# Attention feeding a two-layer network on one core: the value products in 64x64 quarters, in two parts around the next scores

## The chip, the cores and the metric

The kernel runs on one core of a Trainium2 chip. The metric is the device time of one execution in microseconds (us), the median of a few runs; lower is better. The engines are named as in the profile: PE (matrix products; PEld is its weight load), DVE (elementwise and reductions), ACT (activations and copies), POOL (elementwise, selections) and SP (it issues the transfers).

## The reference

Batch 8, 8 heads, sequence 576, head width 64. Each query sees the 128 keys up to and including its own, with a distance bias per head; the result is the input of a network with 512 inputs, 2048 hidden units and 512 outputs.

```python
scores = scale * np.matmul(q, k.transpose(0, 1, 3, 2))
bias = slopes[:, None, None] * (-np.abs(rel).astype(np.float32))[None, :, :]
mask = (rel >= 0) & (rel < window)                    # window = 128
scores = np.where(mask, scores + bias[None], -1000000000.0)
attn = softmax(scores)                                # max, exp, sum, divide
attn_out = np.matmul(attn, v)
x = attn_out.transpose(0, 2, 1, 3).reshape(B * S, H * D)
out = (np.maximum(x @ w_in, 0.0) ** 2) @ w_out
```

## The kernel before, in words

The 4608 tokens are cut into nine chunks of 512, the heads into four pairs. A *couple* q is one chunk and one head pair (q = 4 x chunk + pair, 36 couples); it holds two *segments* of 256 queries, and a segment two groups i of 128 queries for each of the two heads j. A 64-query block sees three 64-key blocks: two of them always in view in whole or in part (the *base*, 128 columns) and one more that shares the place of the block it replaces (the *extra*, 64 columns). The softmax works on a folded 128x128 square per group: `base` copies the base scores from PSUM with ACT, `fold` merges the extra scores under a mask with DVE, then come the row maxima (`top`, DVE), the exponentials (ACT), the sums, and the normalization (`norm`, POOL). `squares` transposes the result on DVE in 32x32 blocks, sends it through DRAM (`way`) and reads it back, and two selections on POOL split it into `own` (keys of the group's own 128-key block) and `prev` (keys of the block before). In `own`, a key only meets queries that stand at or behind it, in `prev` only queries that stand before it in the next block, so one 64x64 quarter of each 128x128 square is all zeros.

The value products (`mix_squares`, L338) multiply those squares with the values: weights of 128 keys x 64 head columns, 128 query columns at a time, two squares added up per group, and the two heads j side by side in the two column halves of the array. `scores` (L392) multiplies 64-row by 64-column pieces of queries and keys, all four quarters of the array in use. The bulk of the work is the network in split precision: `gemm1` (L194) is 12 products of 128x128 weights with 512 columns per hidden block f and chunk, `gemm2` (L223) another 12. ACT takes the Relu from `gemm1`'s bank g, and later steps square and split it.

PSUM has eight banks: two for `sc` (the scores of a couple, S), one for `at` (the value result X), one for `g1` (gemm1's g, and the base scores G of a couple's second segment), four for the accumulators of `gemm2`. Every pool but the last holds one buffer.

The first 150 us or so are ordered by a planner (`start`, with its table of costs and due times); it does the first chunks' attention and the network's chunk 0, and is not touched by the change. From then on PE's order is the written one of the main loop, and the other engines' order comes from a scheduler with priorities. Every eighth half step of the loop holds a *visit*, right behind a `gemm1`: the value products of the old couple q-1 (`back`: `values`, then the copy `high` on ACT and the remainder `low` on DVE, which make that couple's part of the network's input xu), then the scores of the new couple q (`front`), then `gemm2` goes on. Couples 8 to 35 have their value products in such visits: 28 visits, 27 of which also hold the scores of a new couple. In `scores` both heads of the second segment write the one bank G; a POOL no-op (the *turn*) stands between the heads, since the two row halves of the array must not write one bank at a time. A couple whose queries stand at the start of a sequence of 576 has fewer key blocks (`late`); this holds for one or two 64-query blocks of each chunk.

## Time and profile before

| what | value |
|---|---|
| time, median of 3 runs | 956.27 us (956.26 to 956.36) |
| span of the profiled execution, first to last instruction | 954.1 us |
| PE busy | 945.6 us (99%) |
| PEld / DVE / ACT / POOL busy | 795.7 / 499.0 / 417.5 / 215.3 us |
| granted TensorE clock | 1.000 |
| value products, L338 | 1024 records, 63.0 us |
| scores, L392, of the tiles s, g and at | 1648 records |

The profiled execution has no timer of its own beside its span; the timed runs are 2.1 us longer than the span, which is what lies ahead of the first instruction and behind the last. One matrix product of full fp32 stands as two records. A record's duration contains the way through the array, so records overlap; what a piece costs is read from the distance between starts.

### The profile page before, as it was taken

The page shows a single profiled execution, that of the slowest core. Times are in us where ns is not written, and L with a number is a line of the kernel's source. Part 1 is how long each engine was busy: PE and PEld are TensorE (multiplying, and loading weights), DVE is VectorE, ACT ScalarE, POOL GpSimd, SP SyncE. Part 2 cuts the span into 40 slices and gives each one's busy share as a digit, 9 for nine tenths or more (in the row PEclk, how much of TensorE's full clock was granted, in tenths as well). Part 3 has the DMA queues.
Part 4 walks back from the last instruction along what each step waited for, and adds up shares of the span by engine and source line. Part 5 has one row for each costly group of instructions (what it writes and reads, how often), then busy time and mean ns, then how long its engine had stood idle before and what let it go on. Part 6 is the DMA issues. An engine that isn't in the chain of part 4 may idle for free.

```text
span 954.1 us, 17229 instructions
## 1 busy us (share of the span) xinstructions
PE 945.6 (99%) x6388; PEld 795.7 (83%) x6392; DVE 499.0 (52%) x1334; ACT 417.5 (44%) x1107; POOL 215.3 (23%) x254
## 2 busy tenths in 40 slices
PE   9899999999999999999999999999999999999998
PEld 5688888888888888888888888888888888888886
DVE  6998864455545455444544454455555444433222
ACT  7898743333444444434433343344344343332222
POOL 4123331222222222222222222221212222220000
PEclk9999999999999999999999999999999999999999
DMA  9974423322433333222433232333422231111001
GB/s 348 404 274 153 146 68 119 83 66 66 124 85 83 84 88 107 73 77 73 128 83 83 74 110 72 83 83 92 119 71 72 72 96 45 45 45 45 1 1 44
DMA packets 72883, 95.10 MB, mean 100 GB/s; under 512 B 8032, under 2 KB 41952, under 8 KB 72800
## 3 DMA queue, kind: packets, MB, share of 16 engines
q1 hardware_dynamic: 72368, 93.36, 32.9%
q8 instruction: 50, 0.82, 0.4%
q10 hardware_dynamic: 432, 0.66, 0.2%
q14 instruction: 33, 0.27, 0.1%
HBM read 67.76 MB, written 26.21 MB: 98 GB/s over the span
## 4 chain that ended last, share of the span: by engine, by line
PE 95%; DMA 4%; ACT 0%; issue 0%; DVE 0%; SPq 0%; DVEq 0%
PE acc L223 42%; PE g L194 42%; PE at L338 6%; PE s L392 2%; PE g L392 2%; DMA raw<-in_dram 2%; DMA wide<-in_dram 1%; DMA qk<-in_dram 1%; PE at L392 0%; ACT raw L165 0%; ACT t L426 0%; PE acc L291 0%; ACT t L419 0%; ACT o L229 0%; DVE xu L304 0%
## 5 line engine op out<-in xcount | busy, mean ns | idle before, releaser
L194 PE MATMUL g<-xu,w 128*128 128x512 f32 x1728 | 423.2, 394 | 0.8 <-issue 0.8
L194 PEld LDWEIGHTS g<-xu,w 128*128 128x128 f32 x1728 | 344.1, 209 | 56.2 <-issue 1.7
L223 PE MATMUL acc<-hh,w 128*128 128x512 f32 x1152 | 385.9, 396 | 0.0
L223 PEld LDWEIGHTS acc<-hh,w 128*128 128x128 f32 x1152 | 223.9, 194 | 44.6 <-issue 2.4
L207 DVE TENSOR_TENSOR r<-r 128x512 f32<-128x512 f32 x129 | 104.4, 810 | 245.4 <-ACT r L204 244.2
L204 ACT ACTIVATE r<-g 128x512 f32<-128x512 f32 x144 | 85.9, 597 | 325.8 <-PE g L194 322.7
L223 PE MATMUL acc<-hl,w 128*128 128x512 f32 x576 | 226.6, 393 | 0.0
L326 POOL TENSOR_SCALAR_AFFINE_SELECT pp<-pp 128x512 f32<-128x512 f32 x128 | 107.1, 841 | 210.6 <-DMA pp<-way 171.6
L213 DVE TENSOR_TENSOR hl<-r,hh 128x512 fp32r<-128x512 f32 x144 | 109.4, 760 | 68.3 <-ACT hh L211 67.6
L262 POOL TENSOR_TENSOR t<-t,nm 128x512 f32<-128x512 f32 x64 | 82.8, 1294 | 263.5 <-DVE nm L259 155.9
L223 PEld LDWEIGHTS acc<-hl,w 128*128 128x128 f32 x576 | 112.0, 194 | 19.8
L251 ACT ACTIVATE t<-t,nm 128x128 f32<-128x128 f32 x256 | 100.0, 393 | 56.7 <-DVE nm L244 56.6
L211 ACT CAST hh<-r 128x512 fp32r<-128x512 f32 x144 | 89.0, 618 | 76.1 <-DVE r L207 74.5
L438 DVE COPY_PREDICATED t<-cst,s 64x256 f32<-64x256 int32 x100 | 44.5, 445 | 40.8 <-ACT t L426 22.4
L313 DVE STREAM_TRANSPOSE pp<-t 128x512 f32<-128x512 f32 x64 | 45.2, 707 | 38.7 <-POOL t L262 38.5
L338 PEld LDWEIGHTS at<-pp,v 128*64 128x64 f32 x1024 | 55.2, 137 | 11.2 <-issue 10.8
L338 PE MATMUL at<-pp,v 128*64 128x128 f32 x1024 | 63.0, 276 | 0.0
L244 DVE CUSTOM_DVE_ANT_0 t<-t,cst 128x128 f32<-128x128 f32 x256 | 59.0, 293 | 1.0
L251 ACT ACTIVATION_READ_ACCUMULATOR t<-t,nm 128x1 f32 x256 | 48.2, 188 | 0.0
L392 PE MATMUL s<-qk 64*64 64x64 f32 (+2 forms) x1168 | 46.3, 251 | 0.8 <-ACT raw L165 0.8
L392 PEld LDWEIGHTS s<-qk 64*64 64x64 f32 x1168 | 41.9, 133 | 1.0 <-ACT raw L165 1.0
L428 POOL MEMSET t<- 64x128 f32 (+1 forms) x44 | 9.9, 227 | 137.5 <-PE g L392 128.5
(63 smaller groups left out, 472.2 us busy)
## 6 DMA issues: line engine op xcount, KB each, us to landing
raw<-in_dram SPq DMA_DIRECT2D x32, 512.0 KB, 8.7
way<-pp SPq DMA_DIRECT2D x256, 64.0 KB, 1.8
pp<-way SPq DMA_DIRECT2D x64, 256.0 KB, 2.8
qk<-in_dram SPq DMA_DIRECT2D x32, 320.0 KB, 3.5
v<-in_dram SPq DMA_DIRECT2D x32, 320.0 KB, 2.9
qk<-in_dram SPq DMA_DIRECT2D x38, 256.0 KB, 4.1
out_dram<-o SPq DMA_DIRECT2D x35, 256.0 KB, 4.3
v<-in_dram SPq DMA_DIRECT2D x3, 256.0 KB, 4.9
```

What stands on the lines that cost most here:

```text
L194: nc.tensor.matmul(g, w, xs[cc][:, part], start=i == 0, stop=i == 11)
L204: self.relu = nc.scalar.activation(r, g, AF.Relu)
L207: nc.vector.tensor_tensor(r, r, r, op=ALU.mult)
L211: nc.scalar.copy(hh, r)
L213: nc.vector.tensor_tensor(hl, r, hh.bitcast(F32), op=ALU.subtract)
L223: nc.tensor.matmul(self.acc[m], w, h, start=(f == 0 and i == 0), stop=(f == NF - 1 and i == 2))
L244: self.nc.vector.tensor_tensor_reduce(self.t[:, m], self.t[:, m], self.K.nrel(2 * self.p + m // 2), -0.125, BIG, ALU.add, ALU.min, self.nm ...
L251: return self.nc.scalar.activation(self.t[:, m], self.t[:, m], AF.Exp, bias=nm[:, m : m + 1], scale=-1.0, accum_out=nm[:, 4 + m : 5 + m],)
L262: self.nc.gpsimd.tensor_tensor(self.t, self.t, self.nm[:, 8:12].unsqueeze(2).to_broadcast([128, 4, 128]), op=ALU.mult)
L326: nc.gpsimd.affine_select(to, self.own, pattern=[[-32 * sign, 4], [0, 4], [-sign, 32]], compare_op=op, fill=0.0, base=0, channel_multiplie ...
L338: self.nc.tensor.matmul(self.X[r, o : o + 128].rearrange("p (a c) -> p a c", a=4), v[:, 2 * sg + k, r], src[:, :, 2 * j + i], start=sg == ...
L392: mm = nc.tensor.matmul(to, qk[r, q0 : q0 + 64], qk[r, k0 : k0 + 64 * n], start=True, stop=True, skip_group_check=True,)
```

## The change

The visit is written anew as one function, `visit`, for couples 8 to 35.

- The value products go in quarters: 64 keys x 64 head columns as weights, and 64 or 128 query columns. `own` and `prev` are cut by the key half r; for r = 0, `prev` is used for the first 64 queries only and `own` for all 128, for r = 1 `prev` for all and `own` for the last 64. The other quarters, which are zero, are left out. A couple has 32 products for 16 before, with 3072 columns in sum for 2048 before.
- The two row halves of the array write different banks: in the first part, segment 0 takes key half 0 into bank 0 of S, segment 1 key half 1 into bank 1; in the second part the halves change over and add to what stands there. The result X is now columns 0 to 255 of both banks of S.
- The new couple's scores stand between the two parts. Its extra scores go to columns 256 to 511 of S, its base scores, of both segments, to a new two-bank tile `big`. Head j writes bank j. All extras come first, then all bases. The turn (a POOL no-op) now waits for the last extra, and the second part waits for the turn.
- `gemm1` uses the second bank of `big` in place of `g1`; the pools `at` and `g1` are closed when the planner's part is over.
- The copy and the remainder that make xu (`out`) are recorded behind the new couple's base copies and folds, ahead of its maxima; `base` of the first segment now reads `big` and no longer S.

```diff
@@ Kern
+        self.later = ExitStack()
+        pp = lambda name: self.later.enter_context(tc.tile_pool(name=name, bufs=1, space=PSUM))
+        self.at, self.g1 = pp("at"), pp("g1")
+    def join(self, ctx):
+        self.later.close()
+        self.big = ctx.enter_context(self.tc.tile_pool(name="big", bufs=1, space=PSUM))
@@ gemm1
-        g = self.g1.tile([128, 512], F32, name="g")
+        g = self.big.tile([128, 2, 512], F32, name="g")[:, 1] if self.big else self.g1.tile([128, 512], F32, name="g")
@@ Segment
+    def quarters(self, S, r):
+        K, sg = self.K, self.sg
+        v, rows = K.v[self.c, self.p], slice(64 * r, 64 * r + 64)
+        for i in range(2):
+            parts = ((self.prev, 2 * sg + i, 0, 2 + 2 * r), (self.own, 2 * sg + i + 1, 2 * r, 4))
+            for src, k, a, e in parts if r == 0 else parts[::-1]:
+                for j in range(2):
+                    cols = slice(64 * j, 64 * j + 64)
+                    to = S[cols, sg, 128 * i + 32 * a : 128 * i + 32 * e].rearrange("p (a c) -> p a c", c=32)
+                    yield to, v[rows, k, cols], src[rows, a:e, 2 * j + i]
@@ Couple
+    def quarters(self):
...
+                for part, s, i in ((part, s, i) for part in (extra, base) for s in range(2) for i in range(2)):
...
+        for _, j, h, extra, to, q, k, n in sorted(todo, key=lambda y: y[:3]):
+            r = slice(64 * j, 64 * j + 64)
+            yield extra, to, qk[r, q : q + 64], qk[r, k : k + n]
@@ Couple.front
-        self.scores(self.K.g1, "g")
...
-        self.both[0].soft()
@@ Couple
-    def back(self):
-        self.values()
-        self.high()
-        self.low()
+    def out(self, S):
...
+        self.X = S[:, :, 0:256]
...
+def visit(K, old, new):
+    nc, mm = K.nc, K.nc.tensor.matmul
+    S = K.sc.tile([128, 2, 512], F32, name="s")
+    def phase(rows, first):
+        made = []
+        for n, pair in enumerate(zip(*(G.quarters(S, r) for G, r in zip(old.both, rows)))):
+            for to, w, x in pair:
+                made.append(mm(to, w, x, start=first and n < 2, stop=not first, skip_group_check=True))
+        return made
+    last = phase((0, 1), True)[-1]
+    if new:
+        new.S, new.B = S, K.big.tile([128, 2, 512], F32, name="g")
+        for extra, to, w, x in new.quarters():
+            made = mm(to, w, x, start=not extra, stop=True, skip_group_check=True)
+            last = made if extra else last
+    turn = nc.gpsimd.nop()
+    K.tc.add_manual_dep(turn.ins, last.ins.name, SYNC, reason="halves of the keys change banks")
+    for made in phase((1, 0), False)[:2]:
+        K.tc.add_manual_dep(made.ins, turn.ins.name, SYNC, reason="halves of the keys change banks")
+    if new:
+        new.front()
+    old.out(S)
+    if new:
+        new.both[0].soft()
@@ main loop
+        K.join(ctx)
...
-                        if q - 1 in pairs:
-                            pairs.pop(q - 1).back()
...
-                            C.front()
-                            C.turn(0)
...
+                        if q - 1 in pairs:
+                            visit(K, pairs.pop(q - 1), late)
+                        if late:
+                            late.turn(0)
```

How the change moves instructions on PE, in the first visit of the loop: a row is one product or a run of like ones, with the output tile, the inputs, the columns and the count; xu and w are the operands of `gemm1`, pp holds the squares, v the values, qk the queries and keys. Before (the middle of the scores is left out):

```order
L194 MATMUL g<-xu,w_379 128x512 x12
L338 MATMUL at<-pp,v 64x128 x16
L392 MATMUL g<-qk 64x128 x2
L392 MATMUL s<-qk 64x192
L392 MATMUL s<-qk 64x128
L392 MATMUL g<-qk 64x128 x2
...
L392 MATMUL g<-qk 64x128
L392 MATMUL s<-qk 64x64
L223 MATMUL acc<-hh,w_282 128x512
```

And with the change:

```order
L200 MATMUL g<-xu,w_379 128x512 x12
L539 MATMUL s<-pp,v 64x64 x4
L539 MATMUL s<-pp,v 64x128 x4
L539 MATMUL s<-pp,v 64x64 x4
L539 MATMUL s<-pp,v 64x128 x4
L546 MATMUL s<-qk 64x64 x13
L546 MATMUL g<-qk 64x128
L546 MATMUL s<-qk 64x64
L546 MATMUL g<-qk 64x128 x13
L539 MATMUL s<-pp,v 64x64 x4
...
L539 MATMUL s<-pp,v 64x128 x4
L229 MATMUL acc<-hh,w_282 128x512
```

The 16 value products of 128 rows became two groups of 16 quarters, and the scores, which alternated between g and s, now write s first and g behind it.

On ACT, in a visit near the middle of the run (t holds the folded squares, r and hh belong to the network, g and s are the PSUM tiles). Before:

```order
L204 ACTIVATE r_4204<-g_4191 128x512 [waits DVE_49,PE_49]
L211 CAST hh_4205<-r_4204 128x512 [waits DVE_49]
L477 CAST xu_4228<-at_4211 128x512 [waits PE_49]
L426 COPY t_4265<-g_4237 64x2x128 [waits PE_49,Pool_49]
L426 COPY t_4265<-g_4237 128x2x128
L419 COPY t_4263<-s_4236 128x512 [waits DVE_49,PE_49,Pool_49]
L251 ACTIVATE t_4263,nm_4264<-t_4263,nm_4264 128x128 [waits DVE_49,Activation_49]
```

And with the change:

```order
L210 ACTIVATE r_4393<-g_4380 128x512 [waits DVE_49,PE_49]
L217 CAST hh_4394<-r_4393 128x512 [waits DVE_49]
L468 COPY t_4470<-g_4422 64x2x128 [waits PE_49,Pool_49]
L468 COPY t_4470<-g_4422 128x2x128
L461 COPY t_4468<-g_4422 128x512 [waits Pool_49]
L527 CAST xu_4481<-s_4405 128x512 [waits DVE_49,PE_49]
L257 ACTIVATE t_4468,nm_4469<-t_4468,nm_4469 128x128 [waits DVE_49,Activation_49]
```

The copy that makes xu moved from ahead of the base copies to behind them, and waits for DVE's folds; the base copy of the first segment lost its wait for DVE.

On DVE, the same visit with the change, from the last maximum of the first segment on (nm holds maxima and sums):

```order
L250 ISA t_4468,nm_4469<-t_4468,cst_93 128x128
L250 ISA nm_4469 128x1
L528 TENSOR_TENSOR xu_4481<-s_4405,xu_4481 128x512 [waits Activation_49]
L264 TENSOR_SCALAR nm_4469<-nm_4469 128x4 [waits Activation_49]
L265 RECIPROCAL nm_4469<-nm_4469 128x4 [waits DVE_49]
L319 STREAM_TRANSPOSE pp_4495<-t_4468 128x4x4x32 [waits DMAHW2_49,DMAHW3_49,DMAHW1_49,DMAHW7_49,DMAHW0_49,Pool_49]
L213 TENSOR_TENSOR r_4530<-r_4530 128x512 [waits Activation_49]
```

Before, the remainder that makes xu (L480) stood ahead of the folds and the maxima, directly behind the network's own remainder (L213); now it stands behind all eight maxima.

More of the change, by code (lines that the diff above doesn't have):

```diff
@@ L407, in bases @@
     def bases(self, s):
+        parts = lambda x: x.rearrange("p j (i c) -> p j i c", i=2)
+        if self.B is not None:
+            return parts(self.B[:, :, 256 * s : 256 * s + 256]), parts(self.S[:, :, 256 + 128 * s : 384 + 128 * s])
         if s == 0:
@@ L411, in bases @@
             return x[..., 0:128], x[..., 128:192]
-        parts = lambda x: x.rearrange("p j (i c) -> p j i c", i=2)
         return parts(self.G.rearrange("p (j c) -> p j c", j=2)), parts(self.S[:, :, 384:512])
+    def quarters(self):
+        B, S = self.B, self.S
+        todo = []
+        for h in range(2):
+            base, extra = (h, h + 1), (2 - 2 * h,)
+            for j in range(2):
+                at = 0
+                for part, s, i in ((part, s, i) for part in (extra, base) for s in range(2) for i in range(2)):
+                    blocks = [x for x in part if x >= self.both[s].late.get(2 * i + h, 0)]
+                    if not blocks:
+                        continue
+                    n, a = len(blocks), 64 * (blocks[0] - part[0])
+                    if part is extra:
+                        to = S[64 * h : 64 * h + 64, j, 256 + 128 * s + 64 * i : 320 + 128 * s + 64 * i]
+                    else:
+                        to = B[64 * h : 64 * h + 64, j, 256 * s + 128 * i + a : 256 * s + 128 * i + a + 64 * n]
+                    u = 4 * s + 2 * i + h
+                    todo.append((at, j, h, part is extra, to, 64 * u + 640 * s, 256 + 64 * (u + blocks[0]), 64 * n))
+                    at += 64 * n
+        qk = self.K.qk[self.both[0].c, self.both[0].p]
+        for _, j, h, extra, to, q, k, n in sorted(todo, key=lambda y: y[:3]):
+            r = slice(64 * j, 64 * j + 64)
+            yield extra, to, qk[r, q : q + 64], qk[r, k : k + n]
     def base(self, s):
@@ L742, in tile_attn_moe @@
                         if q < 4 * NCH:
[L743 to L746 removed]
+                            late = pairs[q] = Couple(K, q)
+                        if q - 1 in pairs:
+                            visit(K, pairs.pop(q - 1), late)
+                        if late:
+                            late.turn(0)
                 if t % 2 == 0 and n < NF * NCH:
```

11 lines of the change are left out of this document (7 added, 4 removed).

## The prediction

> **What bounds the kernel now.** I read the page first: the share of each engine, the granted clock and the chain of waits.
>
> ```profile
> PE 945.6 (99%) x6388; PEld 795.7 (83%) x6392; DVE 499.0 (52%) x1334; ACT 417.5 (44%) x1107; POOL 215.3 (23%) x254
> PEclk9999999999999999999999999999999999999999
> PE acc L223 42%; PE g L194 42%; PE at L338 6%; PE s L392 2%; PE g L392 2%; DMA raw<-in_dram 2%; DMA wide<-in_dram 1%; DMA qk<-in_dram 1%; PE at L392 0%; ACT raw L165 0%; ACT t L426 0%; PE acc L291 0%; ACT t L419 0%; ACT o L229 0%; DVE xu L304 0%
> ```
>
> PE works without a gap at the full clock, and nearly the whole chain is PE. So the time of the main loop is the sum of PE's own steps: what makes a visit shorter makes the kernel shorter, as long as no new wait comes up on PE. Next I read PE's groups with shapes kept apart, for the tiles in question, and the timeline of PE around one visit.
>
> ```profile
> L338 PE MATMUL at<-pp,v 128*64 128x128 f32 x1024 | 63.0, 276 | 0.0
> L392 PE MATMUL s<-qk 64*64 64x64 f32 x704 | 37.3, 218 | 0.0
> ```
>
> ```profile
> 309.09 2.92 PE L194 MATMUL g<-xu,w 128*128 128x512 f32 x12
> 311.94 1.97 PE L338 MATMUL at<-pp,v 128*64 128x128 f32 x32
> 313.83 0.33 PE L392 MATMUL g<-qk 64*64 64x64 f32 x2
> ...
> 315.21 0.51 PE L223 MATMUL acc<-hh,w 128*128 128x512 f32 x1
> 315.55 0.40 PE L223 MATMUL acc<-hl,w 128*128 128x512 f32 x1
> ```
>
> Neither group waited for anything (0.0). The 32 records of the values take 1.89 us (311.94 to 313.83), the scores 1.38 (to 315.21). A record's 276 or 218 ns holds its way through the array and is no cost; the distance of starts is. Windows cut from the first record of a piece to the first of the next give the values once and the scores once for each of chunks 2 to 8 (there are 3 visits of chunk 2 and 4 of each other; one stands for its chunk).
>
> ```profile
> 157.84:159.73 1.89, 1.89 (x33) 1.72 (x32) 0.69 (x1) 1.03 (x2) 0.00 (x0) 1.00 0.00 0
> 159.73:161.21 1.48, 1.48 (x55) 1.32 (x53) 1.26 (x2) 0.71 (x2) 0.30 (x1) 1.00 0.31 40
> 236.95:238.33 1.38, 1.38 (x55) 1.29 (x53) 1.13 (x2) 0.71 (x2) 0.40 (x2) 1.00 0.23 30
> 339.46:340.92 1.46, 1.46 (x51) 1.31 (x49) 1.21 (x2) 0.70 (x2) 0.30 (x1) 1.00 0.26 46
> 442.15:443.52 1.37, 1.37 (x54) 1.30 (x52) 1.12 (x2) 0.71 (x2) 0.40 (x2) 1.00 0.27 57
> 544.63:546.09 1.46, 1.46 (x51) 1.30 (x49) 1.21 (x2) 0.70 (x2) 0.30 (x1) 1.00 0.27 35
> 647.33:648.80 1.47, 1.47 (x54) 1.39 (x53) 1.23 (x2) 0.70 (x2) 0.20 (x1) 1.00 0.32 56
> 750.29:751.79 1.50, 1.50 (x59) 1.42 (x57) 1.26 (x2) 0.70 (x2) 0.20 (x1) 1.00 0.37 59
> ```
>
> **What a quarter costs.** The scores already run in 64x64 quarters, so their steps price the new value products. PE's timeline in a visit of chunk 8, where g and s take turns in all four quarters:
>
> ```profile
> 750.29 0.33 PE L392 MATMUL g<-qk 64*64 64x128 f32 x2
> ...
> 750.45 0.28 PE L392 MATMUL g<-qk 64*64 64x128 f32 x2
> ...
> 750.66 0.28 PE L392 MATMUL g<-qk 64*64 64x128 f32 x2
> ...
> 751.32 0.23 PE L392 MATMUL s<-qk 64*64 64x64 f32 x2
> ...
> 751.37 0.29 PE L392 MATMUL s<-qk 64*64 64x64 f32 x4
> ...
> 751.49 0.29 PE L392 MATMUL s<-qk 64*64 64x64 f32 x3
> ```
>
> From 750.45 to 750.66 lie two steps of four records of 128 columns: 0.105 us a step. For the values, 16 steps of two records in 1.89 us, less 0.05 for a longer first step (750.29 to 750.45 is 0.16) and 0.10 for the end, give 0.109; I take 0.109. From 751.32 to 751.49 two quarters start six records of 64 columns, three steps: 0.057; I take 0.058. So a step takes as long as its columns, for two tiles of 128x64 and for four of 64x64 alike. Bounds for the 64 columns: 0.055 (half of 128) and 0.109 (no cheaper than 128); the row is at the lower one.
>
> The formula has a check. In the scores each quarter of the array has a stream of its own; the longest decides. A full stream is 768 columns in records of two per product: 4 extras, 2 x 4 x 0.058 = 0.46, and 4 bases, 2 x 4 x 0.109 = 0.87, in sum 1.34. With 0.05 for the first step and 0.11 for the end that is 1.50: chunk 8 has 1.50, chunk 7 1.47. With 704 columns it is 1.22 + 0.16 = 1.38: chunks 3 and 5 have 1.38 and 1.37, but chunks 2, 4 and 6 have 1.48, 1.46, 1.46. I put their 0.08 to 0.10 to the turn between the heads in bank G (an estimate by difference).
>
> **The change part by part.**
>
> *Values.* One part has 16 quarters in four streams: per stream four records of 64 columns and four of 128, 4 x 0.058 + 4 x 0.109 = 0.67. Two parts: 1.34. Before it was 1.89 with its own start and end. The start and end now come once per visit, 0.16, since parts and scores share one shape; the jump from `gemm1` to a visit stays as it is.
>
> *Scores.* All are now split into 64 and 128 columns and no bank is shared, so only the longest stream counts: 1.34 (chunks 7, 8), 1.23 (3, 5: a base of 64 columns for 128), 1.22 (2, 4, 6: an extra is missing).
>
> *Sum per visit*, before less after: chunk 2: 1.89 + 1.48 - (0.16 + 1.34 + 1.22) = 0.65; chunk 3: 3.27 - 2.73 = 0.54; 4: 3.35 - 2.72 = 0.63; 5: 3.26 - 2.73 = 0.53; 6: 0.63; 7: 3.36 - 2.84 = 0.52; 8: 3.39 - 2.84 = 0.55. Over the visits: 3 x 0.65 + 4 x (0.54 + 0.63 + 0.53 + 0.63 + 0.52 + 0.55) = 15.6 us. The last visit has no scores, so its turn lies open between the parts. The turn as it is today, in a visit of chunk 4 (the last record of head 0 in bank G, then the first of head 1):
>
> ```profile
> 337.56 1.97 PE L338 MATMUL at<-pp,v 128*64 128x128 f32 x32
> ...
> 339.85 0.27 PE L392 MATMUL g<-qk 64*64 64x128 f32 x1
> ...
> 340.34 0.32 PE L392 MATMUL g<-qk 64*64 64x128 f32 x1
> ```
>
> 0.49 us from start to start, so 0.4 of wait: 0.05 + 1.34 + 0.4 + 0.11 = 1.90, nothing won there.
>
> *What hides the new waits.* All times from a visit's start, for the first visit of chunk 3 (it starts at 235.06, 1.89 ahead of the window of its scores), where the most hangs on them. ACT, DVE and PE before:
>
> ```profile
> 235.16 0.60 ACT L204 ACTIVATE r<-g 128x512 f32<-128x512 f32 x1 [3.11 <-PE g L194]
> ...
> 238.45 1.03 ACT L426 COPY t<-g 64x128 f32<-64x128 f32 x3 [0.79 <-PE g L392]
> 240.52 0.92 ACT L426 COPY t<-s 128x256 f32<-128x256 f32 x3 [1.04 <-DVE t L438]
> ```
>
> ```profile
> 237.89 0.69 DVE L480 TENSOR_TENSOR xu<-at,xu 128x512 fp32r<-128x512 f32 x1
> 239.51 0.90 DVE L438 COPY_PREDICATED t<-cst,s 64x256 f32<-64x256 int32 x2 [0.92 <-ACT t L426]
> 241.47 0.45 DVE L438 COPY_PREDICATED t<-cst,s 64x256 f32<-64x256 int32 x1 [1.06 <-ACT t L426]
> ...
> 242.47 0.29 DVE L244 CUSTOM_DVE_ANT_0 t<-t,cst 128x128 f32<-128x128 f32 x1
> 242.69 0.08 DVE L244 DVE_READ_ACCUMULATOR2_ANT nm<- 128x1 f32 x1
> ```
>
> ```profile
> 241.24 2.95 PE L194 MATMUL g<-xu,w 128*128 128x512 f32 x12
> ```
>
> (1) The base products write the tile that `gemm1`'s result just left, so they wait for its Relu, which ends at 0.70. Before, the values (1.89) covered that; now the first part (0.72) and three rounds of extras (6 x 0.058) do, to 1.07. Cover left: 0.37; without it the Relu's delay would stand on PE in each visit, with the second part and `gemm2` queued behind. (2) The turn: the last extra starts at about 1.13, plus 0.49 is 1.62; the bases run to 1.95. (3) The next `gemm1` needs the tile back, so both base copies must be done: scores end at 1.95, copies start 0.23 later as now (238.45 against 238.22), 1.03 + 0.92 make 4.1, and the next `gemm1` starts at 6.18 - 0.54 = 5.64. The first segment's copy no longer waits for the fold (1.04 in the row). (4) xu: folds end at 4.17 + 1.00 = 5.17 (241.47 to 242.47), the copy of 0.59 at 5.8, the eight maxima (0.22 each, 242.47 to 242.69) at 6.9, the remainder (0.69) at 7.6. Only in the first visit of a chunk does the next `gemm1` use this xu, its remainder in the eleventh product: 5.64 + 10 x 0.23 (2.95 less the last record's 0.39, over 11 steps) = 7.95. Cover 0.35. (5) The squares of the old couple must be ready at the start of a visit:
>
> ```profile
> 332.02 3.84 POOL L326 TENSOR_SCALAR_AFFINE_SELECT pp<-pp 128x512 f32<-128x512 f32 x4 [5.39 <-DMA pp<-way]
> ```
>
> They end at 335.86, 1.7 ahead of the visit at 337.56. The loop gets some 0.6 shorter per visit, but the chain behind the scores starts 1.3 earlier too, so nothing is late. SP and POOL issue the same work; the loads wait for the end of the visit's PE work and are for a couple two visits on.
>
> So the sum is 15.6 us: the span of 954.1 goes to 938.5. The median of the runs is 2.1 above the span, which the change leaves alone: **940.7 us**.
>
> **The rivals.**
>
> *A wait eats part of it.* Covers (1) and (4) are 0.35 us, and I have drawn them from starts and ends without the handover from engine to engine. If a wait of 0.2 to 0.4 shows in each visit, 27 x 0.3 = 8 us come back: 949. If it shows only at the six chunk starts, 6 x 0.4 = 2.4: 943. For it: two of the covers are thin. Against: they are there. Chance 0.16, most of it small.
>
> *PE's issue becomes the bound.* A visit now issues some 120 products with as many weight loads in 2.7 us, 22 ns a pair; before it was 84 in 3.3, 39 ns. What the trace shows is one burst behind a long wait in the planner's part:
>
> ```profile
> L392 PEld LDWEIGHTS s<-qk x36: 129/133/135, 41.6 to 42.7; 64*64 64x64 f32 x36
> L392 PE MATMUL s<-qk x36: 214/218/344, 41.6 to 42.8; 64*64 64x64 f32 x24, 64*64 64x128 f32 x8, 64*64 64x192 f32 x4
> L392 PE MATMUL at<-qk x12: 267/269/320, 41.7 to 42.8; 64*64 64x128 f32 x12
> ```
>
> 48 pairs in 1.2 us are 25 ns a pair, and that burst may have been bound by its columns. At 25 ns a visit would take 3.0: 27 x 0.3 = 8 us come back, 949. Chance 0.05. The Trainium skill ("TensorE: Matmul & The Clock Gate", section "Wait — 56ns, not 53.3ns?") says that with hardware decoding off the sequencer spends about 62 ns on each matrix product, which would be the bound for small ones. By that rule a visit of 120 products would take an estimated 7.4 us and the kernel would be slower by more than 100; the burst above does not agree with it, so the rule gets no chance of its own.
>
> *Slower: the quarters of the values don't run four at a time.* Unlike the scores, they add to a bank, and two quarters read different 32-column runs of the same rows. If only two of four ran together, a part would take 1.34 and a visit 0.75 longer than before (1.34 lost, 0.59 won): 27 x 0.75 + 1.3 for the last visit = 22 us, 978. It decides from the point where a part takes over 0.96. For it: no row shows an adding quarter. Against: the values before add as well, read the same runs, and keep 0.109. Chance 0.05.
>
> *The change doesn't do what it says*, with the turn or a bank wait holding up each part so that the gain is just used up: 0.6 of new waits per visit, 956. It would take a wait of more than both thin covers together. Chance 0.04.
>
> **How the numbers follow.** The forecast has 0.70, the rivals 0.16, 0.05, 0.05, 0.04. A measurement of this kernel can tell 0.2%, 1.9 us, from no change. Faster: 0.70 + 0.16 + 0.05 = 0.91; the same 0.03; slower 0.06. The range: the lower end is the sum with steps of 0.105 and 0.055, which takes another 0.12 a visit (parts 1.28 for 1.34, scores 0.06 less), 27 x 0.12 = 3.2 us: 937.5. The upper end takes in the waits that eat a part, to 949, with a little less than the full 8 us: 948.0.
>
> **What would show it.** Right: the values' two parts take 0.67 to 0.72 us each, the scores between them 1.2 to 1.35, a visit with scores 2.7 to 2.85, the gap from `gemm1` to the visit and the steps of `gemm1` and `gemm2` are unchanged, and no idle time on PE has ACT, DVE or POOL behind it. Wrong: a first base record that starts later than 1.1 into the visit (Relu), a step in the eleventh product of the first `gemm1` of a chunk (xu), a gap ahead of the second part (turn), or steps of 64 columns over 0.06 (issue, or quarters that take turns). The forecast falls if two adding quarters in one column half can't run together.

## The result, and the profile after

| | before | with the change |
|---|---|---|
| time, median of 4 runs | 956.26 us (956.00 to 956.36) | 941.21 us (940.99 to 941.43) |
| ratio, 95% interval | | 0.984 (0.983 to 0.986): 1.6% faster |
| span of the profiled execution | 954.1 us | 939.7 us |

The forecast was 940.7 us. The profiled execution of the change took 941.43 us. The page of the changed kernel, its line of engine shares and the chain of waits, and the group of the value products:

```profile
PE 930.5 (99%) x7488; PEld 783.0 (83%) x7492; DVE 501.4 (53%) x1334; ACT 416.8 (44%) x1107; POOL 210.6 (22%) x254
PE acc L229 43%; PE g L200 42%; PE s L539 5%; PE g L546 2%; DMA raw<-in_dram 2%; DMA cst<-in_dram 2%; PE s L546 1%; PE at L344 1%; DMA wide<-in_dram 1%; PE s L410 0%; PE at L410 0%; ACT t L468 0%; ACT raw L171 0%; DVE t L480 0%; ACT t L257 0%
L539 PE MATMUL s<-pp,v 64*64 64x128 f32 (+1 forms) x1792 | 52.0, 248 | 0.1
```

PE has 1100 more records than before (7488 against 6388) and is busy 15.1 us less, at the same 99%. The main loop is still the sum of PE's steps. Windows of the changed kernel, from the first value product of a visit to the first `gemm2` product behind it, one visit of each of the chunks 2 to 8 (the first figure is the length, then busy time and records of each engine):

```profile
158.31:161.03 2.72, 2.72 (x121) 2.55 (x120) 1.29 (x2) 1.76 (x4) 0.31 (x1) 1.00 0.00 0
233.53:236.26 2.73, 2.73 (x125) 2.56 (x125) 1.30 (x2) 1.76 (x4) 0.40 (x2) 1.00 0.02 6
334.82:337.54 2.72, 2.72 (x121) 2.55 (x120) 1.30 (x2) 1.74 (x4) 0.31 (x1) 1.00 0.00 0
435.11:437.84 2.73, 2.73 (x125) 2.56 (x125) 1.30 (x2) 1.71 (x4) 0.40 (x2) 1.00 0.00 0
535.30:538.02 2.72, 2.72 (x121) 2.55 (x120) 1.30 (x2) 1.70 (x4) 0.31 (x1) 1.00 0.03 9
635.59:638.42 2.83, 2.83 (x125) 2.66 (x125) 1.39 (x2) 1.71 (x4) 0.20 (x1) 1.00 0.03 6
736.31:739.15 2.84, 2.84 (x129) 2.67 (x128) 1.39 (x2) 1.71 (x4) 0.20 (x1) 1.00 0.02 6
```

Inside a visit, and behind it: PE's timeline of the first visit of chunk 3.

```profile
233.53 0.90 PE L539 MATMUL s<-pp,v 64*64 64x64 f32 x32
234.25 0.57 PE L546 MATMUL s<-qk 64*64 64x64 f32 x26
...
234.72 0.93 PE L546 MATMUL g<-qk 64*64 64x128 f32 x29
...
235.40 0.93 PE L539 MATMUL s<-pp,v 64*64 64x64 f32 x31
236.26 0.51 PE L229 MATMUL acc<-hh,w 128*128 128x512 f32 x1
...
239.14 2.49 PE L200 MATMUL g<-xu,w 128*128 128x512 f32 x10
242.19 0.74 PE L200 MATMUL g<-xu,w 128*128 128x512 f32 x2 [0.56 <-DVE xu L528]
```

The first part takes 0.72 us (233.53 to 234.25), the scores 1.14, the second part 0.86 with the end of the visit in it. The last two rows are the one wait that is new in the whole main loop: the eleventh product of `gemm1` waits for DVE's remainder of xu. The starts of all 28 visits give the account of the two profiled spans, in us:

| | before | with the change |
|---|---|---|
| up to the first visit | 157.84 | 158.31 |
| inside the 28 visits | 92.06 | 76.31 |
| between the visits | 603.46 | 604.33 |
| behind the last visit | 100.80 | 100.76 |

The visits give 15.75 us. Of that, 0.87 is lost between the visits and 0.47 ahead of the first one, in the planner's part, where the two executions are apart from the first microseconds on. The change doesn't touch that part, and in the eight experiments below the first visit starts anywhere from 157.86 to 158.35, so the 0.47 is spread between executions. What is left is 14.4, the difference of the spans.

### The profile page after: what moved, and what is told of

Its sections match the earlier page's. It is cut to its first block, busy times and chain, and to the rows that moved or that the text cites. A ratio compares the mean times of both kernels' runs of the same rounds, so it can differ in the third digit from the quotient of the medians.

```text
span 939.7 us, 19487 instructions
## 1 busy us (share of the span) xinstructions
PE 930.5 (99%) x7488; PEld 783.0 (83%) x7492; DVE 501.4 (53%) x1334; ACT 416.8 (44%) x1107; POOL 210.6 (22%) x254
## 4 chain that ended last, share of the span: by engine, by line
PE 94%; DMA 4%; ACT 1%; DVE 0%; issue 0%; SPq 0%; ACTq 0%; POOLq 0%
PE acc L229 43%; PE g L200 42%; PE s L539 5%; PE g L546 2%; DMA raw<-in_dram 2%; DMA cst<-in_dram 2%; PE s L546 1%; PE at L344 1%; DMA wide<-in_dram 1%; PE s L410 0%; PE at L410 0%; ACT t L468 0%; ACT raw L171 0%; DVE t L480 0%; ACT t L257 0%
## 5 line engine op out<-in xcount | busy, mean ns | idle before, releaser
L213 DVE TENSOR_TENSOR r<-r 128x512 f32<-128x512 f32 x129 | 93.1, 721 | 256.3 <-ACT r L210 256.3
L332 POOL TENSOR_SCALAR_AFFINE_SELECT pp<-pp 128x512 f32<-128x512 f32 x128 | 111.2, 869 | 219.4 <-DMA pp<-way 156.5
L219 DVE TENSOR_TENSOR hl<-r,hh 128x512 fp32r<-128x512 f32 x144 | 119.3, 829 | 74.8 <-ACT hh L217 72.7
L268 POOL TENSOR_TENSOR t<-t,nm 128x512 f32<-128x512 f32 x64 | 73.8, 1154 | 262.1 <-DVE nm L265 234.9
L539 PE MATMUL s<-pp,v 64*64 64x128 f32 (+1 forms) x1792 | 52.0, 248 | 0.1
L539 PEld LDWEIGHTS s<-pp,v 64*64 64x64 f32 x1792 | 40.5, 134 | 10.2 <-issue 9.8
L480 DVE COPY_PREDICATED t<-cst,s 64x256 f32<-64x256 int32 x100 | 44.6, 446 | 6.7 <-ACT t L461 3.6
L527 ACT CAST xu<-s 128x512 fp32r<-128x512 f32 x28 | 16.4, 587 | 41.8 <-DVE t L480 26.8
L468 ACT COPY t<-g 64x256 f32<-64x256 f32 (+2 forms) x86 | 28.0, 340 | 3.8 <-PE g L546 1.0
```

The costliest lines, as they stand in the source:

```text
L213: nc.vector.tensor_tensor(r, r, r, op=ALU.mult)
L219: nc.vector.tensor_tensor(hl, r, hh.bitcast(F32), op=ALU.subtract)
L268: self.nc.gpsimd.tensor_tensor(self.t, self.t, self.nm[:, 8:12].unsqueeze(2).to_broadcast([128, 4, 128]), op=ALU.mult)
L332: nc.gpsimd.affine_select(to, self.own, pattern=[[-32 * sign, 4], [0, 4], [-sign, 32]], compare_op=op, fill=0.0, base=0, channel_multiplie ...
L539: made.append(mm(to, w, x, start=first and n < 2, stop=not first, skip_group_check=True))
```

## The experiments

The theory was the one of the prediction: a visit costs its columns in four streams, and whatever else was lost is a wait for xu at the start of a chunk. In the rows below "rounds" are the times from the start of one visit to the start of the next. Four of the experiments are single executions (the zero quarters, the parts ahead, 64 columns and 32 columns); the others are medians of 4 to 10.

**What the wait in chunk 3 is.** ACT and DVE in the changed kernel, the same visit (it starts at 233.53):

```profile
235.71 1.84 ACT L468 COPY t<-g 64x128 f32<-64x128 f32 x6
239.68 0.59 ACT L527 CAST xu<-s 128x512 fp32r<-128x512 f32 x1 [2.13 <-DVE t L484]
```

```profile
237.58 0.30 DVE L484 COPY_PREDICATED t<-cst 64x128 f32<-64x128 int32 x1 [1.24 <-ACT t L468]
237.90 1.35 DVE L480 COPY_PREDICATED t<-cst,s 64x256 f32<-64x256 int32 x3
239.28 0.31 DVE L484 COPY_PREDICATED t<-cst,s 64x128 f32<-64x128 int32 x1
239.62 0.29 DVE L250 CUSTOM_DVE_ANT_0 t<-t,cst 128x128 f32<-128x128 f32 x1
...
241.44 0.69 DVE L528 TENSOR_TENSOR xu<-s,xu 128x512 fp32r<-128x512 f32 x1
```

DVE starts with a fold of the couple's first segment (L484, 237.58). It can only run when both base copies are done, and the folds of the second segment, whose copy is done earlier, stand behind it. So all folds end at 239.59, 6.06 into the visit; the remainder ends at 242.13, 8.60 into it. The eleventh product was due at 7.95. The first experiment puts the second segment's folds first, the second puts xu's remainder ahead of the eight maxima; neither touches PE's program.

```diff
-                nc.vector.copy_predicated(d, mask..., e)
+                self.behind(s, nc.vector.copy_predicated(d, mask..., e))
...
+    def behind(self, s, made):
+        if s == 1:
+            self.folds = getattr(self, "folds", []) + [made]
+        elif self.B is not None:
+            for x in self.folds:
+                self.K.tc.add_manual_dep(made.ins, x.ins.name, ORDER, reason="second segment's folds first")
```

> The change, with one order added on DVE: the folds of a new couple's first segment come behind those of its second segment (before the change they stood so in every visit; with the change the scheduler put one fold of the first segment ahead in chunks 2 and 3). Nothing is left out. My theory: the one wait of PE on DVE that the change brought (0.56 us idle shown, in the first visit of chunk 3, ahead of the eleventh product of gemm1) comes from that fold, which waits for both base copies and holds up the fold behind it; with the order mended the folds end at about 5.15 us into the visit instead of 6.05, the remainder of xu at 7.7 instead of 8.6, ahead of the 7.95 at which it is needed. So the wait goes, and with it the whole excess of 1.0 us of that round of the loop: 940.2 against 941.2. The rival, that the remainder is late because of its place behind the eight maxima, expects the wait to stay: 941.2.

DVE and PE with that order, in the first visit of chunk 3 (at 233.37):

```profile
236.60 1.36 DVE L480 COPY_PREDICATED t<-cst,s 64x256 f32<-64x256 int32 x3 [0.42 <-ACT t L468]
...
240.33 0.69 DVE L535 TENSOR_TENSOR xu<-s,xu 128x512 fp32r<-128x512 f32 x1
```

```profile
238.97 2.96 PE L200 MATMUL g<-xu,w 128*128 128x512 f32 x12
```

The folds start 3.23 into the visit, the remainder ends at 7.65, and the twelve products run through. The round is 25.05 us, where it was 26.12, so the rival, which expected the wait to stay, doesn't hold. The time is 940.43 us (940.07 to 940.50), ratio 0.9835 (0.9822 to 0.9848). Between the visits 603.47 us are left, 0.86 less than in the change. Not all of the wait's 1.07 came back, since one round of chunk 7 is now 25.45 instead of 25.18, without any wait in it; more on that at the end.

```diff
-        self.nc.vector.tensor_tensor(halves(self.u[:, 1]), ..., op=ALU.subtract)
+        return self.nc.vector.tensor_tensor(halves(self.u[:, 1]), ..., op=ALU.subtract)
...
-            self.top(m)
+            x = self.top(m)
+            if getattr(self, "low", None) is not None:
+                self.K.tc.add_manual_dep(x.ins, self.low.ins.name, ORDER, reason="a chunk's last remainder first")
...
-    old.out(S)
+    low = old.out(S)
     if new:
+        for G in new.both:
+            G.low = low if new.both[0].p == 0 else None
```

> The change, with one order added on DVE: in the first visit of a chunk, all eight maxima of the new couple come behind the remainder that makes xu. Nothing is left out, and the folds keep the order of the change. My theory: the remainder then ends 1.7 us earlier, at about 6.9 us into the first visit of chunk 3 and 6.1 to 6.5 in the others, so that no chunk start waits on DVE (the fold order alone had mended chunk 3, but its round in chunk 7 became 0.27 us longer); the exponentials start up to 1.4 us later in six visits, which the next gemm1 still covers. So every round of the loop takes its shortest time: 1.04 us less than the change, 940.2, with no wait of PE on DVE. The rival, that the exponentials then hold up the next Relu and PE with it, expects 941 or more, with PE waiting on ACT.

```profile
240.20 0.69 DVE L530 TENSOR_TENSOR xu<-s,xu 128x512 fp32r<-128x512 f32 x1 [0.71 <-ACT xu L529]
```

Here the first segment's fold still comes first, but the remainder ends at 7.43 after the visit's start (233.46), and no round is longer than its neighbours: 603.23 us between the visits. The 7.43 is later than the 6.9 that was expected, as the remainder itself waits 0.71 us for the copy on ACT; in chunks 4 to 8 it ends at 6.2 to 6.7. The time is 940.61 us (940.17 to 942.29), ratio 0.9841 (0.9826 to 0.9855), the span 938.5. Two different cures of one delay remove the same wait, so it was this delay. In the medians they are 0.8 and 0.6 us below the change's 941.21. With the folds in order all five executions (940.07 to 940.50) lie below all four of the change (940.99 to 941.43); with the remainder first one of four doesn't (942.29), so there the gain is plain only in the rounds.

The second cure has a price that its time doesn't show. In the first visit of a chunk it starts the maxima 1.1 to 1.3 us later than in the change, and with them all that follows up to the squares, which the next visit needs. POOL's last selection of them then ends only 0.09 to 1.33 us ahead of that visit, where in the change it is 0.66 to 2.70.

**What the zero quarters are worth.** The quarters without content are multiplied again, with the change's form otherwise:

```diff
-            parts = ((self.prev, 2 * sg + i, 0, 2 + 2 * r), (self.own, 2 * sg + i + 1, 2 * r, 4))
+            parts = ((self.prev, 2 * sg + i, 0, 4), (self.own, 2 * sg + i + 1, 0, 4))
```

> The change with the zero quarters kept: each part has 128 columns in every product (4096 columns a couple for 3072), all else alike; the products with zeros change nothing in the result. If a part costs its columns, it takes 8 steps of 0.109 = 0.87 us for 0.67, so 28 visits x 2 x 0.20 = 11.4 us more: about 952.6, and of the gain of 15 us only the 4 from one start and end per visit and from the scores are left. The rival, that the gain comes from the shape and the merged start alone and zero quarters were free, expects 941.

The time was 953.81 us, 1.2 over the 952.6 that was expected, and the rival's 941 is out. An undisturbed visit takes 3.130 us instead of 2.724, 0.406 more, which over 28 visits is 11.4. The rest stands in one visit, in which PE waits for POOL:

```profile
337.17 0.43 PE L539 MATMUL s<-pp,v 64*64 64x128 f32 x2
338.65 0.99 PE L539 MATMUL s<-pp,v 64*64 64x128 f32 x27 [1.06 <-POOL pp L332]
```

```profile
337.07 1.52 POOL L332 TENSOR_SCALAR_AFFINE_SELECT pp<-pp 128x512 f32<-128x512 f32 x2 [5.97 <-DMA pp<-way]
```

POOL's last two selections of the squares, which in the change end at 332.12, waited 5.97 us for their load and began only with the visit; that costs 1.48 us from start to start. The wait in chunk 3 was there as in the change. Why the load came late can be read a little earlier on POOL and DVE:

```profile
328.69 0.73 POOL L332 TENSOR_SCALAR_AFFINE_SELECT pp<-pp 128x512 f32<-128x512 f32 x1 [6.66 <-DMA pp<-way]
329.39 1.04 POOL L268 TENSOR_TENSOR t<-t,nm 128x512 f32<-128x512 f32 x1
```

```profile
330.46 0.71 DVE L319 STREAM_TRANSPOSE pp<-t 128x512 f32<-128x512 f32 x1 [5.73 <-POOL t L268]
```

In this one round POOL does a selection of the first segment ahead of the normalization of the second (L268). The selection waits 6.66 us for its load, the normalization stands behind it, and the transposition, the way through DRAM and the load of the second segment all follow late. In the change, and in every other round of this run, both normalizations come ahead of the selections. It is the same kind of fault as the fold in chunk 3, an order of the scheduler on an engine that isn't the bottleneck; no run turned this order back. So of the 15.7 us that the visits give, 11.4 are the zero quarters, and the rest is the form: one start and end per visit in place of two, and the scores.

**What the place of the scores is worth.** Both parts ahead, the scores behind them:

```diff
-    last = phase((0, 1), True)[-1]
-    if new:
-        ...
+    last = phase((1, 0), True)[-1]
     turn = nc.gpsimd.nop()
     K.tc.add_manual_dep(turn.ins, last.ins.name, SYNC, reason="halves of the keys change banks")
-    for made in phase((1, 0), False)[:2]:
+    for made in phase((0, 1), False)[:2]:
         K.tc.add_manual_dep(made.ins, turn.ins.name, SYNC, reason="halves of the keys change banks")
     if new:
+        new.S, new.B = S, K.big.tile([128, 2, 512], F32, name="g")
+        for extra, to, w, x in new.quarters():
+            mm(to, w, x, start=not extra, stop=True, skip_group_check=True)
+    if new:
         new.front()
```

> The change with both parts of the value products ahead of the scores (the key halves in the other order, so that the scores can follow in the same banks), the turn between the parts with nothing beside it. Same products, same columns. My theory: the turn costs 0.49 us from the start of the last record of the first part to the first of the second, 0.37 to 0.43 of it open, in each of 27 visits: 10 to 11.6 us more, 951 to 953. The rival, that PE passes the turn without a gap (its queue goes on), expects 941.2.

A visit of chunk 2:

```profile
183.76 1.94 PE L539 MATMUL s<-pp,v 64*64 64x64 f32 x64
185.52 0.57 PE L550 MATMUL s<-qk 64*64 64x64 f32 x26
...
186.85 0.51 PE L229 MATMUL acc<-hh,w 128*128 128x512 f32 x1
```

The parts take 1.76 us together (183.76 to 185.52), with nothing between them. Two parts at 0.67 and 0.05 for the first step make 1.39, so the open turn costs 0.37, as expected, though the starts around it are 0.41 apart and not 0.49: some 0.05 of the 0.37 is a second longer first step behind the turn. The visits are 9.94 us longer in sum, 0.37 for each of 27. Between the visits another 1.80 us are lost: each first round of a chunk from 3 on is 0.2 to 0.8 longer than the next ones, as the scores now end later and xu with them (PE's waits name the remainder of xu in two of these rounds). The expectation left that out, and the time, 953.76 us, lies above its 951 to 953. The rival, that PE passes the turn without a gap, doesn't hold. So the turn, left open, would use up 9.9 of the 15.7 us that the visits give; in the change the scores cover it fully, since no visit with scores shows a wait there.

**What the values alone and the scores alone are worth.** The values are computed as before the change, in 128 rows, but into the shared tile and with the scores as changed:

```diff
-    last = phase((0, 1), True)[-1]
+    for G in old.both:
+        G.X = S[:, G.sg, 0:256]
+        G.mix_squares()
...
-    for made in phase((1, 0), False)[:2]:
-        K.tc.add_manual_dep(made.ins, turn.ins.name, SYNC, reason="halves of the keys change banks")
```

> The change with the value products as they were (128 keys by 64 columns, zeros and all, ahead of the scores, no turn in the visit), but with its scores: extras first, two-bank base tile, no turn between the heads. It measures the scores apart. My theory: values 1.89 as before; the scores take 0.16 plus the longest stream, so 1.38 in chunks 2, 4 and 6 (before 1.48, 1.46, 1.46: the turn between the heads is gone), 1.39 in 3 and 5 (1.38, 1.37), 1.50 in 7 and 8 (1.47, 1.50): 27 visits together 0.7 us faster, 955.5. The rival, that the 0.08 to 0.10 in chunks 2, 4 and 6 were not the turn but the order of the pieces in the streams, expects them to stay: 956.5.

The scores take 1.38 to 1.39 in chunks 2 to 6 and 1.50 in 7 and 8, where the kernel before has 1.48, 1.38, 1.46, 1.37 and 1.46 in chunks 2 to 6 and 1.47 and 1.50 behind them: the dear chunks 2, 4 and 6 came down to the formula, and the visits in sum are 0.60 us shorter than before, for 0.7 expected. The rival, that these chunks stay dear, doesn't hold as it was put; but the new scores have no turn and another order of their pieces at once, so which of the two made them dear isn't shown. And yet the time is not the 955.5 expected but 957.81 us (957.30 to 958.68), ratio 1.0019 (1.0010 to 1.0028). The main loop's waits on PE:

```profile
PE g L200 <- DVE xu L528: 0.5, 2, 0.2
```

The first round of chunk 3 takes 26.41 us instead of 25.65, and those of chunks 4, 5, 7 and 8 are also 0.2 to 0.5 longer; 605.77 us lie between the visits instead of 603.46. Visits that save 0.6 stand against 2.3 lost between them. If the late xu is the cause, the remainder ahead of the maxima must bring it back:

```diff
-    last = phase((0, 1), True)[-1]
+    for G in old.both:
+        G.X = S[:, G.sg, 0:256]
+        G.mix_squares()
...
-    old.out(S)
+    low = old.out(S)
     if new:
+        for G in new.both:
+            G.low = low if new.both[0].p == 0 else None
```

> The kernel with the value products as they were and the new scores, which came out at 957.8 although its visits are 0.6 us shorter in sum than before, with the same order added: in the first visit of a chunk the remainder comes ahead of the maxima. My theory: its loss was made of waits on xu at the six chunk starts (rounds 0.3 to 0.8 us longer than the others of their chunk); with the remainder early they go, and 955.6 is left, 0.6 under before. The rival, that something else in the new order costs the 2.2 us, expects 957.5 or more.

It brings back 2.16 of the 2.3: 603.61 us between the visits, and the main loop's list of PE's waits is empty. So the late xu was the cause. The time is 956.31 us (955.95 to 957.07), ratio 1.0003 (0.9993 to 1.0012), and not the expected 955.6, 0.6 under the kernel before. Three visits have longer values, by 0.27, 0.08 and 0.03. The weight loads of the worst of them:

```profile
261.33 1.29 PEld L344 LDWEIGHTS s<-pp,v 128*64 128x64 f32 x24 [0.29 <-POOL pp L332]
```

Again it is the squares that were late. All three visits are the second of their chunk, directly behind the one in which the maxima stand behind the remainder, so this is the price of that order once more. The scores' new form alone is worth 0.6 us at most, and in both runs the later work on the other engines took it away.

**Whether issue is a bound.** The same columns in more and shorter products: 64 columns each (24 instead of 16 products per part, 48 records), and 32 columns (96 records):

```diff
-                for j in range(2):
-                    cols = slice(64 * j, 64 * j + 64)
-                    to = S[cols, sg, 128 * i + 32 * a : 128 * i + 32 * e]...
-                    yield to, v[rows, k, cols], src[rows, a:e, 2 * j + i]
+                for b in range(a, e, 2):
+                    for j in range(2):
+                        cols = slice(64 * j, 64 * j + 64)
+                        to = S[cols, sg, 128 * i + 32 * b : 128 * i + 32 * (b + 2)]...
+                        yield to, v[rows, k, cols], src[rows, b : b + 2, 2 * j + i]
```

> The change with every value product cut to 64 columns: 48 products a couple for 32, the same columns, so some 152 pairs of load and product in a visit. If a step costs its columns, a stream has 12 records of 0.058 a part, 0.70 us for 0.67: 28 x 2 x 0.03 = 1.6 us more, a span of 941.3. If PE's issue bounds at 25 ns a pair, a visit takes 152 x 25 ns = 3.8 us for 2.7, which makes 30 us more: a span of 969.

> The change with every value product cut to 32 columns: 96 products a couple, the same columns, some 250 pairs in a visit. If a step costs its columns alone (0.031 us), a part takes 24 x 0.031 = 0.74 us: 28 x 2 x 0.07 = 4 us more, a span of 944. If a record can't be shorter than one of about 64 columns, a part takes 24 x 0.058 = 1.39: 40 us more, 980. If issue bounds at 25 ns a pair, 250 pairs take 6.2 us for 2.7: some 95 us more, 1035. The Trainium skill ("TensorEngine Tiling (Array Packing)", section "Instruction Overhead") says that a product of one column takes as long as one of 60, which would give the middle one of these.

They took 948.22 and 1011.19 us (spans of 946.5 and 1009.5), in neither case a number that was expected. The trace parts each into two. First, undisturbed visits; the first part in the first visit of chunk 2, with 64 columns and with 32:

```profile
158.15 0.93 PE L540 MATMUL s<-pp,v 64*64 64x64 f32 x48
158.90 0.57 PE L547 MATMUL s<-qk 64*64 64x64 f32 x26
```

```profile
158.33 1.60 PE L540 MATMUL s<-pp,v 64*64 64x32 f32 x96
159.75 0.60 PE L547 MATMUL s<-qk 64*64 64x64 f32 x26
```

48 records take 0.75 us, 15.6 ns a pair of load and product, 0.03 more than the 32 records of the change. 96 take 1.42, 14.8 ns a pair, or 0.059 for each record in its quarter. A record of 32 columns is thus as long as one of 64 (0.058): there is a floor, and the change's short records lie on it. With 64 columns a quarter's next load starts 2 ns behind its product, hidden under it; with 32 it starts some 30 ns behind, and the next product 28 ns behind the load, so that four loads and four products take turns, 6.7 ns from start to start within a group. Whether the floor is one of the record or of the issue (15 ns a pair) these runs can't tell, since four quarters at 0.059 are 15 ns a pair. The Trainium skill ("TensorEngine Tiling (Array Packing)", section "Instruction Overhead") says that each product has a fixed overhead of some 60 cycles, so that a product of 1 column takes as long as one of 60; for 32 against 64 columns the trace agrees (0.059 and 0.058); no run here has fewer columns. By this floor alone the 32 columns cost 1.43 a visit (4.155 against 2.724).

Second, visits in which PE stands still. The main loop's waits on PE, for 64 columns and for 32:

```profile
PE s L540 <- issue: 2.5, 3, 0.9
PE s L540 <- POOL pp L332: 1.6, 2, 1.0
```

```profile
PE s L540 <- issue: 13.5, 17, 1.0
PE s L540 <- POOL pp L332: 4.4, 3, 1.9
PE acc L229 <- issue: 1.5, 3, 0.7
PE g L547 <- issue: 0.9, 1, 0.9
```

With 64 columns the visits are 7.42 us longer in sum than in the change: 28 times 0.057 are 1.6, the expected cost of the columns, and 5.8 stand in the three visits with these waits (idle time, and the starts that come apart around it). With 32 columns they are 68.6 longer: about 40 by the floor, the rest by such stops, and only five visits keep to the length that the floor gives. The waits on POOL, two and three, are in those visits in which POOL has the order of the zero-quarter run. "issue" is time for which the profile shows no cause. One visit of the 64-column kernel, and the transfers around it:

```profile
288.24 0.96 PE L540 MATMUL s<-pp,v 64*64 64x64 f32 x41
289.97 0.34 PE L540 MATMUL s<-pp,v 64*64 64x64 f32 x6 [0.77 <-issue]
```

```profile
q8 instruction: 1, 0.02, 11.6%
```

The second row is from the stretch from 287.0 to 287.6: the only packet of the queue for instructions near this visit starts at 287.25, 2.7 us before PE goes on. In all three stops of this kernel PE goes on 2.63 to 2.72 us after the start of such a packet, in all 23 in the main loop of the 32-column kernel 2.3 to 2.9 after. That PE had run out of instructions fits this; no run moved the fetches, so it is argued and not shown.

## Why the prediction was right

The time, 941.21, is 0.5 above the forecast of 940.7, and its mechanism and sizes hold: the visits save 15.75 us for 15.6 predicted. That the total comes so near is in part chance: 0.87 us was lost between the visits and 0.47 ahead of them, and 0.4 came back outside the span. By the prediction's steps:

- **The values.** A first part of 0.72 is the predicted 0.05 + 0.67. The steps of 64 columns at 0.058 and of 128 at 0.109 hold for products that add, with four quarters at work (the row that gave the 0.058 had two): the starts in one quarter are 0.056 to 0.058 apart behind 64 columns and 0.109 to 0.112 behind 128. The zero quarters were 11.4 of the gain by the experiment.
- **The scores and the sum.** The visits measured 2.72, 2.73, 2.72, 2.73, 2.72, 2.83 and 2.84; the prediction's were 2.72, 2.73, 2.72, 2.73, 2.72, 2.84 and 2.84. The 0.08 to 0.10 that it put down, by difference, to the turn between the heads are gone with the new scores, also where these alone were changed; that it was the turn and not the old order of the pieces stays an estimate. By starts, the scores take 1.12 to 1.14 in chunks 2 to 7 and 1.24 in chunk 8, less than the 1.2 that the prediction named as a sign in all but the last: the second part begins in quarters whose scores are done while others still have columns. It is the sum over the longest stream that holds, not the borders between the pieces.
- **The last visit.** Expected 1.90 with the turn of 0.4 open; measured 1.87 against 1.90 before, and the experiment with both parts ahead shows an open turn of 0.37.

```profile
837.09 1.94 PE L539 MATMUL s<-pp,v 64*64 64x64 f32 x64
838.96 0.51 PE L229 MATMUL acc<-hh,w 128*128 128x512 f32 x1
```

- **Covers (1), (2), (3).** No visit with scores shows a wait for the Relu, the turn or the tile of the base products. The first base record starts 1.08 into the visit, where 1.07 was predicted; only in chunk 8 it is 1.19, past the sign of 1.1, and there a fourth round of extras stands ahead of it (0.72 + 8 x 0.058 = 1.18), not the Relu.
- **Cover (4) failed in one place of six.** The remainder of xu ends 7.44 to 7.82 after the visit's start in the first visits of chunks 4 to 8, where 7.6 was predicted, and nobody waits. In chunk 3, where the prediction drew its sum, it ends at 8.60. The step that failed is "folds end at 4.17 + 1.00": it took the folds in the order of the kernel before, in which no fold of the first segment held them up, and with the change that order is another. They end at 6.06. So the sign that the prediction named for xu, a step at the eleventh product, showed there, and the rival *a wait eats part of it* came true at one chunk start of six, with 1.07 us in place of the six times 0.4 it was given. Its thin cover was named rightly; what was missing is the order on DVE ahead of it.
- **Cover (5).** The squares are never late in the change; the least that POOL's last selection ends ahead of a visit is 0.7 us. The 1.7 that the prediction quoted was that of one visit: in the kernel before the least is 0.4 (the second visit of chunk 7). In four of the variants the squares are late, by POOL's order in three of them and by the later maxima in the fourth. So "nothing is late" came true, but the working had no ground for it beyond that one visit, and here luck had a share.
- **Issue.** There is no stop for issue in the main loop of the change; this is all that the waits of PE show there:

```profile
PE g L200 <- DVE xu L528: 0.6, 1, 0.6
```

  The 25 ns a pair that the rival took from the planner's burst was no limit: pairs can follow each other every 15 ns, and the change needs 22. The rule of about 62 ns a product with hardware decoding off, in the Trainium skill ("TensorE: Matmul & The Clock Gate", section "Wait — 56ns, not 53.3ns?"), doesn't agree with these 15 ns; how the products are decoded here no run shows.
- **Quarters that take turns.** They don't: 32 records of 16 adding quarters in 0.72 us are four at a time.
- **The base time.** 2.1 us lay around the span before; around that of the change lie 1.7 (941.43 less 939.7), so that the 14.4 us of the spans became 14.8 there. It isn't the change that did it: the executions of the kernel before that ran beside the experiments have 1.7 too (956.03 with a span of 954.3), so the 2.1 was that of one execution.

## What to carry to other kernels

On an engine without idle time, price a rearrangement by the longest stream in its columns, from steps of the same shape in the same trace; that held here to 1% in the sum over 28 visits. Then check every cover in the new order of all engines, not in the old one, and at each place where it is thin: one fold ahead of others on DVE cost 1.07 us of PE, and the same chain took more than the whole gain from the version with only the scores changed. A cure is itself a new order: the remainder ahead of the maxima healed one wait and left the squares 0.09 us of cover. Cutting products shorter has a floor, and near it other limits come up that a shorter program never shows.

## What the runs showed of the hardware that was not expected

- **A floor per product.** With four quarters at work, records of 32 columns take as long as those of 64: 0.059 and 0.058 us, 15 ns a pair of load and product.
- **PE's program itself is loaded in pieces.** The pages count the packets of the queue for instructions, before, with the change and with 32 columns:

```profile
q8 instruction: 50, 0.82, 0.4%
```

```profile
q8 instruction: 59, 0.97, 0.4%
```

```profile
q8 instruction: 87, 1.43, 0.6%
```

A packet has 16 KB (0.97 MB over 59), and the changed kernel has 7488 + 7492 records on PE, 254 for each packet; the other two come to 256 and 255. A visit of the change with scores starts 240 to 256 records, products and loads together, in 2.72 to 2.84 us, one packet's worth in about the time that lies between a packet's start and the end of a stop (2.3 to 2.9). With 304 to 320 records in 2.78 to 2.90 us (64 columns) three visits have such a stop. The change may thus be close to a limit that no wait of its own shows.
- **The pace of long products changes for a round.** After the wait in chunk 3 the next groups of twelve 512-column products take 2.80 us instead of 2.76, up to the next visit; this is 0.2 of the 1.07 us lost. In the run with the folds reordered one round of chunk 7 has this pace, 25.45 us for 25.18, without any wait ahead of it. In the run with the scores alone changed it follows the waits in chunks 3, 4 and 8 and makes up 0.7 of the 2.3 us lost there. What sets it is open.
